# Moving the decoding of the second network's weights from steps 15 to 59 to steps 60 to 95

## The chip, the core and the metric

The kernel runs on one core of a Trainium2 chip. The core has five engines that run beside each other, each through its own list of instructions in order: TensorE (PE in the rows, with its weight loads as PEld), VectorE (DVE), ScalarE (ACT), GpSimd (POOL) and SyncE (SP), which issues most DMA transfers. Time is device time in microseconds from one launch. The kernel before took 1014.66 us, the median of three runs (1014.65, 1014.66 and 1016.03 us).

## What is computed

Four sequences of 4224 tokens with 192 channels go through three layers, shortened here from the reference:

```
x  = causal convolution of x, 7 taps per head, softmax weights       # 8 heads of 24 channels
u  = x + ((x^T @ U) @ V)^T                                           # rank 32, along the sequence
x  = u + max(u @ w_ch1, 0) @ w_ch2                                   # first network, 192 -> 768 -> 192
u  = x + real(fft over tokens and channels of x)
un = (u - mean(u)) / sqrt(var(u) + 1e-6)
y  = u + max(un @ moe2_w_ch1, 0) @ moe2_w_ch2                        # second network, same sizes
```

All inputs arrive as 64-bit floats. A weight is therefore loaded as two 32-bit words and decoded on the chip, scaled by the largest absolute value, and split into a high and a low 16-bit part. Products are formed from high x high, high x low and low x high.

## The kernel before

**Blocks and steps.** A sequence is cut into 11 blocks of 384 tokens. Each block goes once through the first network and once through the second, which gives 88 blocks; their order over (network, sequence) is (0,0), (0,1), (0,2), (1,0), (0,3), (1,1), (1,2), (1,3). So blocks 0 to 32 use the first network, and block 33 is the first that needs the weights of the second. A block i is worked in three steps, 3i, 3i+1 and 3i+2. In each step two of the six 128-row parts of layer 1 are issued (`layer1`, L665 and L655: five matmuls a part, then the eviction `hh` on ACT at L650 and the residue `hl` on VectorE at L651), and one third of layer 2 of the block before (`layer2`, L697 to L701, 18 matmuls, added to the result by VectorE at L704).

**Paired blocks.** In blocks 5 to 10, 22 to 33 and 76 to 87 all six parts of layer 1 are issued in the first step, and the six evictions follow together. All matmul results use one ring of eight PSUM buffers, taken in turn. After the six parts of layer 1 only two buffers are left, so the third group of matmuls after them waits until the first `hl` of the block has been written.

**Preparing the next input.** While block i runs, the input of block i+2 is prepared. VectorE adds a product (L525 or L534), takes maxima (L712) and scales (`cmax`, `rc`, L547 and L550); ACT scales and rounds (`un` L555, `sp` L578); GpSimd subtracts (`sp` L561); a transposing DMA issued by SP (L585) writes `ch`, which the matmuls at L665 read. In the paired stretches ACT's share of this stands between `rc` and the evictions of the next block.

**Background work.** Other work is written as lists of small functions, here called units. A table of windows `[a, z, units]` spreads the n units of a list over steps a to z-1: unit k is issued at the end of step a + floor(k (z-a) / n). Units of one step are issued in the order of the table: tables, weights of the second network (`weights_units(1)`), convolution of sequence 2 (`conv_units(2)`), the transform of sequence 0 (`fft_units`), and so on. An engine meets a unit's instructions at that place of its list and can't pass them by.

**The units that the change touches.** `weights_units(1)` first issues three DMA loads of 2.3 MB together (L201, `load`), then twelve decodes (`dec`: five VectorE instructions at L172 to L179 on 128x192 words, and a maximum at L223), and between and after them the scaling (L230 to L250) and the splits (L255, L262 on GpSimd, copies at L286 to L296). `conv_units` for sequences 2 and 3 loads its input in halves (`load_x`, L159), convolves (L398) in place, and ends with a scaling of its rank-32 product (`gsplit`). In the first list of `fft_units` a unit of kind a holds fold(c+1) and the matmuls s33(c,0), a unit of kind m holds split33(c+1) and s33(c,1); gathers of rows (`loadx`, indirect DMAs of GpSimd at L756) go with both. Fold is three instructions of VectorE (L790 to L793) and one of GpSimd (L795). Split33 is two of ACT (L802, L803) and one of GpSimd (L804), which s33 (L823) waits for. The two writers of `z` behind s33, ACT at L830 and VectorE at L831, wait for each other in turn where a unit writes `z` twice.

Of the kernel before, what the change touches and what calls it, by code (L numbers as in the profile page):

```python
# [19 lines left out]
FF = 768  # L20
# [77 lines left out]
def build(tc, io):  # L98
# [30 lines left out]
    with tc.manual_schedule():  # L129
# [59 lines left out]
        def weights_units(i):  # L189
            st = {}  # L190
            FH = FF // 2
            NW = FF + FH + NM * D
# [33 lines left out]
            def scale(n):  # L226

                mx = st["mx"]
                o, c = (0, len(pieces[0])) if n == 0 else (len(pieces[0]), len(pieces[1]))
                nc.vector.tensor_reduce(out=mx[:, 16 + n:17 + n], in_=mx[:, o:o + c], axis=AX.X,  # L230
                                        op=ALU.max)
# [72 lines left out]
            def decs(n):  # L304
                o = len(pieces[0]) if n else 0
                return [lambda q=q, e=e: dec(*q, o + e) for e, q in enumerate(pieces[n])]

            if i == 0:
                st["part"] = load_part
                w0_st.update(st=st)  # L310
            return [load] + decs(0) + [lambda: scale(0), lambda: scale2(0),
                                       lambda: scaled(0, FF + FH, 0), split1h, split1e, split1a, split1b] + \
                   decs(1) + [lambda: scale(1), lambda: scale2(1),
# [16 lines left out]
        def gsplit(b, gf):  # L330

            st = {}

            def size():
                gm = st["gm"] = wrk.tile([P, 4], F32, name="gm", bufs=2)
                nc.vector.tensor_reduce(out=gm[:, 0:1], in_=gf(), axis=AX.X, op=ALU.max,
                                        apply_absolute_value=True)

            def scale():
                gm = st["gm"]  # L340
                all_max(gm[:, 1:2], gm[:, 0:1])
                nc.vector.tensor_scalar(out=gm[:, 1:2], in0=gm[:, 1:2], scalar1=1e-30,
                                        scalar2=1 / 64.0, op0=ALU.max, op1=ALU.mult)
                nc.vector.reciprocal(gm[:, 2:3], gm[:, 1:2])
                nc.vector.tensor_tensor(out=gm[:, 3:4], in0=gm[:, 1:2], in1=vsc[:, 0:1],
                                        op=ALU.mult)

            def split():
                gm = st["gm"]
                g = wrk.tile([P, D], F16, name="gst", bufs=2)  # L350
                nc.scalar.activation(g[:96], gf()[:96], AF.Identity, scale=gm[:96, 2:3])
                nc.vector.scalar_tensor_tensor(out=g[64:96], in0=gf()[64:96],
                                               scalar=gm[64:96, 2:3], in1=g[64:96],
                                               op0=ALU.mult, op1=ALU.subtract)
                gst[b] = g, gm

            return [size, scale, split]

        def conv_units(b):
            st = {}  # L360
# [79 lines left out]
            if not b:  # L440
                return out

            return out + [lambda f=f: (f(), stored and stored.pop(0)())
                          for f in gsplit(b, lambda: st["g"])]

        def z_tile():
# [278 lines left out]
        def fft_units(b):  # L725
# [6 lines left out]
            def scale():  # L732

                m = xmax[b]
                nc.vector.tensor_reduce(out=m[:, 11:12], in_=m[:, 0:NB], axis=AX.X, op=ALU.max)
# [177 lines left out]
                nc.gpsimd.tensor_tensor(out=y1, in0=y1, in1=near(1, 1), op=ALU.add)  # L913

            last = len(chunks) - 1
            first = [lambda: (scale(), loadx(0)), scale2, lambda: (fold(0), loadx(1)), lambda: split33(0), None]
            for c in range(len(chunks)):
                a, m = [lambda c=c: s33(c, 0)], [lambda c=c: s33(c, 1)]
                if c < last:
# [100 lines left out]
        def play(t):  # L1020
            for q in START[t].split() if t < len(START) else ():
                if q in jobs:
                    jobs[q]()
                else:
# [13 lines left out]
        ft = [fft_units(b) for b in range(B)]  # L1038

        windows = [[28, 32, [load_tables]],  # L1040
                   [15, 60, weights_units(1)],
                   [25, 57, [lambda: load_x(2, 0, 0), lambda: load_x(2, 0, 1), None] + conv_units(2)],
                   [37, 70, ft[0][0]], [70, 100, ft[0][1]],
                   [98, 127, ft[1][0]], [125, 153, ft[1][1]],
# [93 lines left out]
```

## Time and profile before

| what | value |
| --- | --- |
| median of three runs | 1014.66 us |
| profiled execution, span from the first to the last instruction | 1017.3 us |
| profiled execution, a time of its own beside the span | none is given |
| TensorE busy | 979.1 us, 96% of the span |
| VectorE busy | 748.4 us, 74% |
| ScalarE busy | 604.4 us, 59% |
| GpSimd busy | 380.9 us, 37% |
| mean granted clock of TensorE | 0.992 |

The profile is of one execution. A row's times count from the start of its span. Its busy shares are averages over stretches that have different limits, so the table says only that TensorE comes first. Where it stood idle, and for whom, is in the rows further below.

### The profile page before, as it was taken

The page shows a single profiled execution, that of the slowest core. Times are in us where ns is not written, and L with a number is a line of the kernel's source. Part 1 is how long each engine was busy: PE and PEld are TensorE (multiplying, and loading weights), DVE is VectorE, ACT ScalarE, POOL GpSimd, SP SyncE. Part 2 cuts the span into 40 slices and gives each one's busy share as a digit, 9 for nine tenths or more (in the row PEclk, how much of TensorE's full clock was granted, in tenths as well). Part 3 has the DMA queues.
Part 4 walks back from the last instruction along what each step waited for, and adds up shares of the span by engine and source line. Part 5 has one row for each costly group of instructions (what it writes and reads, how often), then busy time and mean ns, then how long its engine had stood idle before and what let it go on. Part 6 is the DMA issues. An engine that isn't in the chain of part 4 may idle for free.

```text
span 1017.3 us, 25682 instructions
## 1 busy us (share of the span) xinstructions
PE 979.1 (96%) x9929; PEld 764.8 (75%) x9929; DVE 748.4 (74%) x2094; ACT 604.4 (59%) x1512; POOL 380.9 (37%) x397
## 2 busy tenths in 40 slices
PE   8789898999899999999999999998999999999998
PEld 5466676777677777877778887776888877877776
DVE  7766577689876656687776777897789787766663
ACT  2556554765676666656576666655656665555552
POOL 0111111253552344265534445564157651562110
PEclk9999999999999999999999999999999999999999
DMA  7596857685536666443425455433344332542332
GB/s 288 155 230 183 252 148 189 178 213 158 151 99 154 203 201 179 114 138 101 102 73 146 134 155 139 108 87 82 87 131 110 107 87 65 137 110 68 82 72 63
DMA packets 190804, 139.28 MB, mean 137 GB/s; under 512 B 128186, under 2 KB 164257, under 8 KB 189913
## 3 DMA queue, kind: packets, MB, share of 16 engines
q1 hardware_dynamic: 183095, 124.59, 45.6%
q0 software_dynamic: 7104, 12.70, 4.8%
q8 instruction: 77, 1.26, 0.5%
q14 instruction: 46, 0.38, 0.1%
q10 hardware_dynamic: 482, 0.35, 0.1%
HBM read 61.69 MB, written 46.11 MB: 106 GB/s over the span
## 4 chain that ended last, share of the span: by engine, by line
PE 62%; DVE 12%; DMA 11%; POOL 5%; issue 5%; ACT 4%; SPq 0%; DVEq 0%; ACTq 0%; POOLq 0%
PE l L665 24%; PE l L697 9%; PE l L701 8%; PE l L699 8%; PE l L655 5%; DMA ch<-sp 4%; DVE hl L651 3%; DMA xm<-x2d,mrow 2%; POOL xm L756 2%; PE cv L398 2%; PE sd L863 2%; PE s L879 2%; DMA x1d<-xw 1%; DVE x L790 1%; POOL xp L804 1%
## 5 line engine op out<-in xcount | busy, mean ns | idle before, releaser
L665 PE MATMUL l<-ch,w1h 128*128 128x384 f16 x1584 | 407.2, 327 | 15.4 <-DMA ch<-sp 10.1
L697 PE MATMUL l<-w2h,hh 128*128 128x192 f16 x1584 | 391.9, 247 | 5.8 <-DVE hl L651 4.5
L699 PE MATMUL l<-w2l,hh 128*128 128x192 f16 x1584 | 391.4, 247 | 1.2 <-DVE w2l L264 1.2
L701 PE MATMUL l<-w2h,hl 128*128 128x192 f16 x1584 | 391.4, 247 | 0.5 <-DVE hl L651 0.4
L651 DVE SCALAR_TENSOR_TENSOR hl<-l,hh 128x384 f16<-128x384 f32 x528 | 267.6, 549 | 127.2 <-ACT hh L650 126.1
L650 ACT ACTIVATE hh<-l 128x384 f16<-128x384 f32 x528 | 235.3, 494 | 155.7 <-PE l L655 155.3
L665 PEld LDWEIGHTS <-w1h 128*128 128x128 f16 x1584 | 155.1, 98 | 106.8 <-DMA ch<-sp 12.3
L697 PEld LDWEIGHTS <-hh 128*128 128x128 f16 x1584 | 155.6, 98 | 23.1 <-issue 12.3
L665 PE MATMUL l<-ch,w1l 128*128 128x384 f16 x528 | 172.7, 327 | 0.0
L699 PEld LDWEIGHTS <-hh 128*128 128x128 f16 x1584 | 155.7, 98 | 17.1 <-issue 6.5
L701 PEld LDWEIGHTS <-hl 128*128 128x128 f16 x1584 | 155.7, 98 | 3.1 <-DVE hl L651 1.4
L561 POOL TENSOR_TENSOR sp<-un,sp 128x576 f16<-128x576 f32 x44 | 57.3, 1302 | 250.4 <-ACT sp L578 228.3
L655 PE MATMUL l<-ch,w1l 128*128 128x384 f16 (+1 forms) x528 | 133.9, 327 | 0.0
L756 POOL DMA_INDIRECT xm<-x2d,mrow x84 | 84.9, 1011 | 21.3 <-issue 17.8
L631 POOL TENSOR_TENSOR sp<-un,sp 128x576 f16<-128x576 f32 x34 | 44.9, 1320 | 120.2 <-ACT sp L578 118.9
L625 ACT ACTIVATE un<-u,mr,rs 128x192 f32<-128x192 f32 x132 | 62.4, 537 | 25.3 <-DVE mr L619 24.7
L555 ACT ACTIVATE un<-u,rc 128x192 f32<-128x192 f32 x132 | 50.2, 445 | 43.0 <-DVE rc L550 43.0
L704 DVE SCALAR_TENSOR_TENSOR u<-l,cmax,u 128x192 f32<-128x192 f32 x132 | 54.5, 413 | 25.5 <-PE l L701 20.9
L665 PEld LDWEIGHTS <-w1l 128*128 128x128 f16 x528 | 51.8, 98 | 28.0 <-issue 4.0
L543 ACT ACTIVATE junk<-u 128x192 f16<-128x192 f32 x132 | 47.7, 361 | 40.6 <-DVE u L534 24.2
L849 POOL DMA_INDIRECT u<-x2d,mrow x64 | 62.4, 975 | 15.3 <-issue 11.7
L704 DVE SCALAR_TENSOR_TENSOR u<-l,ws,u 128x192 f32<-128x192 f32 x132 | 53.9, 410 | 18.2 <-PE l L701 18.0
(136 smaller groups left out, 1189.5 us busy)
## 6 DMA issues: line engine op xcount, KB each, us to landing
x2d<-u SPq DMA_DIRECT2D x68, 288.0 KB
u<-x1d SPq DMA_DIRECT2D x44, 288.0 KB
out_d<-u SPq DMA_DIRECT2D x43, 288.0 KB
x1d<-xw SPq DMA_DIRECT2D x36, 210.0 KB
u<-x2d SPq DMA_DIRECT2D x32, 192.0 KB
x<-x2d SPq DMA_DIRECT2D x60, 99.0 KB
xw<-x_d SPq DMA_DIRECT2D x4, 1344.0 KB
xw<-x_d SPq DMA_DIRECT2D x8, 672.0 KB
```

What stands on the lines that cost most here:

```text
L561: low_engine(0, b, j).tensor_tensor(out=sp[:, :, D:2 * D], in0=k["un"], in1=sp[:, :, :D], op=ALU.subtract)
L625: nc.scalar.activation(un[:, t], u[:, t], AF.Identity, scale=k["r"][:, t:t + 1], bias=k["m"][:, t:t + 1])
L650: nc.scalar.activation(hh[:, m], acc[m], AF.Relu)
L651: nc.vector.scalar_tensor_tensor(out=hl[:, m], in0=acc[m], scalar=0.0, in1=hh[:, m], op0=ALU.max, op1=ALU.subtract)
L655: nc.tensor.matmul(acc[m].rearrange("p (r n) -> p r n", r=TB), lhsT=w["l1"][rows, n, m * P:(m + 1) * P], rhs=kd[x][rows], start=False, sto ...
L665: nc.tensor.matmul(o, lhsT=w[v][:, e, ms], rhs=kd[x], start=(n == 0), stop=False)
L697: nc.tensor.matmul(o, lhsT=hh[:, m, rs], rhs=w["h2"][:, m], start=(m == 0), stop=False)
L699: nc.tensor.matmul(o, lhsT=hh[:, m, rs], rhs=w["l2"][:, m], start=False, stop=False)
L701: nc.tensor.matmul(o, lhsT=hl[:, m, rs], rhs=w["h2"][:, m], start=False, stop=(m == NM - 1))
L704: nc.vector.scalar_tensor_tensor(out=u[:, r], in0=o, scalar=sc, in1=u[:, r], op0=ALU.mult, op1=ALU.add)
L756: nc.gpsimd.indirect_dma_start(out=xs[c][1][:, g], out_offset=None, in_=x2d[b][:], in_offset=bass.IndirectOffsetOnAxis(ap=mrow[:99, k:k + ...
L849: nc.gpsimd.indirect_dma_start(out=u2[:, s0 + 2 * e], out_offset=None, in_=src[:], in_offset=bass.IndirectOffsetOnAxis(ap=mrow[:, k2 + e - ...
```

## The change

Four edits. The window of the second network's weights becomes steps 60 to 95. Its units get a new order: four empty units behind the loads, the decodes of the second half between the later units of the first, and three empty units near the end; 24 units become 31. The scaling at the end of the convolution of sequences 2 and 3 gets two empty units, so that these two lists have 18 units for 16. In the first list of each transform an empty unit stands between finding the largest value and using it, which makes 18 units of 17. Nothing else is computed and nothing is left out.

```diff
@@ weights_units @@
+            if i:
+                d0, d1 = decs(0), decs(1)
+                return [load, None, None, None, None] + d0 + \
+                    [lambda: scale(0), d1[0], d1[1], lambda: scale2(0), d1[2],
+                     lambda: scaled(0, FF + FH, 0), split1h, split1e, d1[3], split1a, d1[4],
+                     split1b, d1[5], lambda: scale(1), None, None, lambda: scale2(1), None,
+                     lambda: scaled(FF + FH, NW, 1), split2]
             return [load] + decs(0) + [lambda: scale(0), lambda: scale2(0),
                                        lambda: scaled(0, FF + FH, 0), split1h, split1e, split1a, split1b] + \
                    decs(1) + [lambda: scale(1), lambda: scale2(1),
...
@@ gsplit @@
-            return [size, scale, split]
+            return [size, None, scale, None, split] if b > 1 else [size, scale, split]
...
@@ conv_units @@
-            return out + [lambda f=f: (f(), stored and stored.pop(0)())
+            return out + [lambda f=f: (f and f(), stored and stored.pop(0)())
...
@@ fft_units @@
-            first = [lambda: (scale(), loadx(0)), scale2, lambda: (fold(0), loadx(1)), lambda: split33(0), None]
+            first = [lambda: (scale(), loadx(0)), None, scale2, lambda: (fold(0), loadx(1)), lambda: split33(0), None]
...
@@ windows @@
-                   [15, 60, weights_units(1)],
+                   [60, 96, weights_units(1)],
```

By the rule for windows the loads move from step 15 to 60. The decodes stood at steps 16, 18, 20, 22, 24, 26, 41, 43, 45, 46, 48 and 50; now they stand at 65, 66, 68, 69, 70, 71, 73, 75, 77, 82, 84 and 86. The last split moves from step 58 to 94. Line numbers below the first edit grow by 7.

First place: VectorE in block 6 of the kernel before, from the copy of a convolution's product to the maximum at L712. `dec` is the decoder's scratch, `u_1474` the loaded weights, `l` a PSUM result of layer 2.

```order
L419 COPY gacc<-gp 128x192
L704 SCALAR_TENSOR_TENSOR u<-l_1505,cmax,u 128x192
L172 TENSOR_SCALAR dec<-u_1474 128x192
L175 TENSOR_SCALAR dec<-dec 128x192
L176 TENSOR_SCALAR dec<-dec 128x192
L178 SCALAR_TENSOR_TENSOR dec<-u_1474,dec 128x192
L179 SCALAR_TENSOR_TENSOR u_1474<-u_1474,dec 128x192
L223 TENSOR_REDUCE mx_1482<-u_1474 128x1
L122 TENSOR_REDUCE vsc<-am 128x1
```

The same place of VectorE in the changed kernel.

```order
L426 COPY gacc<-gp 128x192
L711 SCALAR_TENSOR_TENSOR u<-l_1495,cmax,u 128x192
L122 TENSOR_REDUCE vsc<-am 128x1
L471 TENSOR_SCALAR vsc<-vsc 128x1
L473 RECIPROCAL vsc<-vsc 128x1
L711 SCALAR_TENSOR_TENSOR u<-l_1536,cmax,u 128x192
L719 TENSOR_REDUCE xmax<-u 128x1
```

The first decode and its wait for the load are gone from the path to the maximum.

Second place: VectorE at the end of block 22 before, from the second third of layer 2 to the first `hl` of block 23.

```order
L704 SCALAR_TENSOR_TENSOR u<-l_4649,cmax,u 128x192
L534 SCALAR_TENSOR_TENSOR u<-h,gm,u 128x192
L704 SCALAR_TENSOR_TENSOR u<-l_4674,cmax,u 128x192
L712 TENSOR_REDUCE xmax<-u 128x1
L547 TENSOR_SCALAR cmax<-cmax 128x3
L550 RECIPROCAL rc<-cmax 128x3
L831 SCALAR_TENSOR_TENSOR z<-s_4699,z 95x34x3
L831 SCALAR_TENSOR_TENSOR z<-s_4699,z 95x34
L651 SCALAR_TENSOR_TENSOR hl<-l_4725,hh 128x384
```

The same place in the changed kernel, from the last third of layer 2 on.

```order
L711 SCALAR_TENSOR_TENSOR u<-l_4570,cmax,u 128x192
L719 TENSOR_REDUCE xmax<-u 128x1
L554 TENSOR_SCALAR cmax<-cmax 128x3
L557 RECIPROCAL rc<-cmax 128x3
L172 TENSOR_SCALAR dec<-u_4133 128x192
L175 TENSOR_SCALAR dec<-dec 128x192
L176 TENSOR_SCALAR dec<-dec 128x192
L178 SCALAR_TENSOR_TENSOR dec<-u_4133,dec 128x192
L179 SCALAR_TENSOR_TENSOR u_4133<-u_4133,dec 128x192
L223 TENSOR_REDUCE mx_4141<-u_4133 128x1
L838 SCALAR_TENSOR_TENSOR z<-s_4602,z 95x34x3
L838 SCALAR_TENSOR_TENSOR z<-s_4602,z 95x34
```

A decode now stands between `rc` and the two writes of `z` (step 68); another one, of step 66, stands ahead of these rows, behind the first third of layer 2.

Third place: SP's queue around the end of block 10 before. The second load of `xw` here is the second half of chunk 1 of sequence 2.

```order
L504 DMA u<-x1d_67 128x576
L159 DMA xw<-x_d 128x1344
L716 DMA x2d_70<-u 128x576
L504 DMA u<-x1d_67 128x576
L585 DMA_TRANSPOSE ch<-sp 128x9x128
L159 DMA xw<-x_d 128x1344
L716 DMA x2d_70<-u 128x576
```

The same place in the changed kernel.

```order
L511 DMA u<-x1d_67 128x576
L159 DMA xw<-x_d 128x1344
L723 DMA x2d_70<-u 128x576
L159 DMA xw<-x_d 128x1344
L511 DMA u<-x1d_67 128x576
L592 DMA_TRANSPOSE ch<-sp 128x9x128
L159 DMA xw<-x_d 128x960
```

The half moves up past one load of `u` and one transpose; it is issued at step 32 for 33 before, and the convolution that reads it is issued at step 33 for 35 before.

## Rows read from the trace of the kernel before

**Rows 1.** The page's first part: busy time, share of the span and instructions.
```profile
PE 979.1 (96%) x9929; PEld 764.8 (75%) x9929; DVE 748.4 (74%) x2094; ACT 604.4 (59%) x1512; POOL 380.9 (37%) x397
```
**Rows 2.** Timeline of TensorE: start, us, instruction, [idle before <-releaser]; five waits.
```profile
124.86 0.32 PE L697 MATMUL l<-w2h,hh 128*128 128x192 f16 x1 [3.37 <-DVE hl L651]
...
165.34 0.24 PE L697 MATMUL l<-w2h,hh 128*128 128x192 f16 x1 [1.16 <-DVE hl L651]
...
169.74 0.34 PE L665 MATMUL l<-ch,w1h 128*128 128x384 f16 x1 [1.18 <-DMA ch<-sp]
...
193.02 0.72 PE L398 MATMUL cv<-xw,tap 64*64 64x168 f32 x12 [1.03 <-DMA xw<-x_d]
...
267.08 0.50 PE L665 MATMUL l<-ch,w1h 128*128 128x384 f16 x1 [2.83 <-DMA ch<-sp]
```
**Rows 3.** Windows: us, busy PE, PEld, DVE, ACT, POOL (x), PEclk, DMA share, GB/s.
```profile
122.00:126.00 4.00, 1.14 (x8) 1.05 (x8) 1.75 (x4) 3.97 (x12) 1.27 (x1) 0.65 0.52 192
126.00:130.00 4.00, 4.00 (x36) 2.83 (x35) 3.19 (x7) 1.78 (x4) 0.26 (x1) 0.50 0.98 227
...
268.00:272.00 4.00, 4.00 (x30) 2.91 (x29) 1.80 (x7) 2.13 (x6) 0.61 (x1) 0.75 0.62 207
...
694.00:698.00 4.00, 4.00 (x27) 2.75 (x26) 1.80 (x4) 1.41 (x4) 1.83 (x2) 0.67 0.57 145
```
**Rows 4.** Timeline of VectorE: the wait for the load; start and end of one decode.
```profile
117.57 0.26 DVE L172 TENSOR_SCALAR dec<-u 128x192 int32<-128x192 int32 x1 [3.41 <-DMA u<-wa_d]
...
156.61 0.25 DVE L172 TENSOR_SCALAR dec<-u 128x192 int32<-128x192 int32 x1
...
158.54 0.28 DVE L122 TENSOR_REDUCE gm<-am 128x1 f32<-128x128 f32 x1
```
**Rows 5.** Timeline of ACT in block 9, behind that decode.
```profile
164.23 1.61 ACT L650 ACTIVATE hh<-l 128x384 f16<-128x384 f32 x4
```
**Rows 6.** Timeline of GpSimd ahead of the wait for `ch` at 267.08.
```profile
258.68 1.23 POOL L795 TENSOR_TENSOR xm<-x 99x380 f32<-99x380 f32 x1 [6.43 <-DVE xm L791]
...
262.44 1.30 POOL L561 TENSOR_TENSOR sp<-un,sp 128x576 f16<-128x576 f32 x1
```
**Rows 7.** Timeline of TensorE: waits in the transform of sequence 2.
```profile
678.71 0.48 PE L823 MATMUL s<-vt,xp 99*97 99x102 f16 x6 [1.16 <-POOL xp L804]
...
690.84 0.29 PE L823 MATMUL s<-vt,xp 99*97 99x102 f16 x2 [1.17 <-ACT xp L803]
692.56 0.62 PE L823 MATMUL s<-vt,xp 99*97 99x102 f16 x9 [1.43 <-POOL xp L804]
```
**Rows 8.** Timelines of SP's queue and of TensorE in block 11.
```profile
181.42 0.32 SPq L716 DMA_DIRECT2D x2d<-u  x1
...
187.93 0.58 SPq L159 DMA_DIRECT2D xw<-x_d  x1
...
184.14 0.72 PE L398 MATMUL cv<-xw,tap 64*64 64x168 f32 x12
```
**Rows 9.** Windows of 20 us, columns as in rows 3, in blocks 22 to 26.
```profile
320.00:340.00 20.00, 19.54 (x200) 15.19 (x198) 13.18 (x36) 12.33 (x38) 6.92 (x8) 1.00 0.68 178
340.00:360.00 20.00, 20.00 (x214) 15.26 (x215) 12.42 (x32) 14.45 (x42) 8.26 (x12) 1.00 0.57 179
```
**Rows 10.** Timelines of ACT, VectorE and TensorE between blocks 22 and 23.
```profile
323.42 0.32 ACT L830 ACTIVATE z<-s 95x34 f16<-95x34 f32 x1 [0.87 <-DVE z L831]
...
326.01 0.87 ACT L650 ACTIVATE hh<-l 128x384 f16<-128x384 f32 x2 [0.39 <-PE l L655]
...
326.53 2.88 DVE L651 SCALAR_TENSOR_TENSOR hl<-l,hh 128x384 f16<-128x384 f32 x6 [2.46 <-ACT hh L650]
...
327.90 0.25 PE L697 MATMUL l<-w2h,hh 128*128 128x192 f16 x1
```
**Rows 11.** Timelines of GpSimd and VectorE: a decode beside a GpSimd subtraction.
```profile
248.12 1.64 POOL L804 TENSOR_TENSOR xp<-xm,xp 99x768 f16<-99x768 f32 x1 [0.42 <-POOL sp L561]
...
248.15 1.72 DVE L176 TENSOR_SCALAR dec<-dec 128x192 int32<-128x192 int32 x1
```

## The prediction

> **What bounds the kernel now.** I read the page first, then TensorE's waits, then short windows around the long ones, and last the chains that led to them. The page gives TensorE 979.1 us of a span of 1017.3 us [rows 1], so the time can only fall where TensorE stands idle or runs at its lower clock. The waits tell where that is. Behind the start-up, the large ones of the first network lie in blocks 6 to 18: 3.37, 1.16, 1.18, 1.03 and 2.83 us [rows 2]. Those of the second network that matter here lie in blocks 55 and 56: 1.16, 1.17 and 1.43 us [rows 7]. A long wait costs twice. After the one of 3.37 us the granted clock is 0.65 and then 0.50 of full speed for 4 us each; after the one of 2.83 us it is 0.75, and after the pair in block 56 it is 0.67 [rows 3]. Half speed is the lower of the two levels, 1.2 GHz for 2.4. In blocks 22 to 26, into which the decodes move, TensorE is nearly full (19.54 and 20.00 of 20 us) and VectorE has about a third of the time free (13.18 and 12.42 busy) [rows 9].
>
> **What goes away.** The decode at 117.57 sat at the head of VectorE's queue for 3.41 us until its weights landed [rows 4]. Behind it waited the addition that frees layer 2's buffers, the scales, ACT's rounding, the evictions, and then TensorE for 3.37 us. This wait leaves that place with its decode. With it goes the slow clock: from 124.86 to 130 TensorE works 5.1 us at half speed [rows 2, 3], which loses 2.6. Sum 6.0 us.
>
> One decode holds VectorE from 156.61 to 158.54, that is 1.93 us [rows 4]. In block 9 it stands ahead of the scales, so `hh` comes at 164.23 [rows 5], TensorE waits 1.16 us for the residue and then 1.18 us for the next `ch` [rows 2]. Two microseconds earlier, both are covered: 2.3 us.
>
> The wait at 267.08 has a longer chain. GpSimd's fold stood 6.43 us waiting for VectorE, whose queue held a decode of 1.93 us ahead of the fold, and the subtraction that makes `ch` came behind it, at 262.44 [rows 6]. Without decodes the fold is earlier, and by the new step numbers (fold at step 51 for 50, the subtraction before it in that step) it no longer stands ahead of that subtraction. 2.83 us of wait, and 1.0 us for the 2 us at half speed in the window 268 to 272 [rows 3]: 3.8 us.
>
> In the transform of sequence 2 the old list had split33 and the s33 that reads it one step apart at steps 169 and 170, where 1.17 + 1.43 us were lost [rows 7]. With 18 units in 27 steps each unit m stands two steps ahead of the next a. The loss of 1.16 us a block earlier has the same cause, a late `xp`, but had two steps already. With the slow clock behind it (0.67 over 4 us is 2.6 us at half speed, 1.3 lost [rows 3]) 5.1 us are at stake, and I take 5.0. Gains together: 6.0 + 2.3 + 3.8 + 5.0 = 17.1 us.
>
> **What comes instead: the decodes in blocks 22 to 28.** Each one placed ahead of `rc`, or ahead of VectorE's part of `z`, delays ACT's rounding and so the evictions of the next block. ACT waited 0.39 us for TensorE ahead of them, and the first residue, about a sixth of 2.88 us after 326.53, was written near 327.05, while TensorE reached the matmul that needs its buffer at 327.90 [rows 10]: 0.85 us more. A delay of d costs TensorE d - 0.39 - 0.85. Block 22 has two such decodes, of steps 66 and 68. The second follows `rc`, but the row at 323.42 shows ACT waiting for VectorE between two writes of `z` [rows 10], and that pair is now behind it. So 3.9 - 1.24 = 2.7 us at the start of block 23. A wait of 2.83 us brought the low clock [rows 2, 3], so 1.4 us more, as after that wait. Block 23 has three decodes, two ahead of `rc`: 2.7 again, less 0.5 since a slower TensorE leaves VectorE time, 2.2. Block 24 has one: 0.7. The last five, the three scalings and splits on ACT and the subtractions on GpSimd lie in longer blocks with convolutions, where VectorE has 7.6 of 20 us free [rows 9]; I take 1.3. Bounds: nothing, if VectorE's free third covers all, and 12 x 1.9 = 23 us, if every decode were to lengthen TensorE's path by its whole length. I take 2.7 + 1.4 + 2.2 + 0.7 + 1.3 = 8.3, near the rows of block 9, where one decode cost 2.3.
>
> **The loads at step 60** share the DMA engines with `ch` of block 21, whose transpose is issued ahead of them. Before, they ran without a wait for `ch` on TensorE; I take 0.3 us (0 to 2). The first decode now comes five steps later than they, so it does not wait.
>
> **The convolution of sequence 2.** The half of its input that the convolution in block 11 needs is issued earlier in SP's list, right behind the store at 181.42 instead of at 187.93; there it landed just ahead of 193.02, 5 us later [rows 2, 8]. So it lands near 187, and later if the store ahead of it counts. But the convolution itself moves up two steps, to the place at 184.14 [rows 8]. TensorE waits about 3.1 us for 1.03 before, and may fall to the low clock (half of 1.6): 2.1 + 0.8 = 2.9 us.
>
> **The other transforms.** For sequence 0 the distances stay two steps. Sequence 1 keeps two places with one step. Sequence 3 had none and gets three (202 to 203, 205 to 206, 208 to 209). Such a place cost 2.60 us at step 170 [rows 7]; three others of before show little. Bounds 0 to 7.8; I take 1.5.
>
> **Sum.** Losses 8.3 + 0.3 + 2.9 + 1.5 = 13.0, gains 17.1: 4.1 us less. The profiled execution has no time beside its span of 1017.3, which lies 2.6 above the median; the difference carries over: 1014.66 - 4.1 = 1010.6 us.
>
> **A rule that speaks against the change.** Beside a GpSimd subtraction that began at 248.12, an instruction of a decode took 1.72 us [rows 11], where the first of a decode without such a neighbour took 0.25 [rows 4]. The Trainium skill ("SBUF — State Buffer", section "SBUF: two separate sides") says that the ports GpSimd shares with VectorE are an exclusive lock: whoever begins first keeps it to its end, and the other waits. The trace agrees. Taken over to all decodes it makes the rival named third below.
>
> **Rivals.** First, VectorE's free third hides the decodes: the losses fall to 0.3 + 2.9 + 1.5 = 4.7 us. That gives 1014.66 - 17.1 + 4.7 = 1002.3. For it: 6.8 us of 20 free [rows 9]; against: block 9 did not hide one. Second, gains and losses cancel: only the wait for the load goes (6.0), and the fold and the transforms find new late steps, at 1014.5. For it: those chains pass GpSimd, which the change relieves little. Third, GpSimd holds the decodes: the last five lie where it works 8.26 us of 20 [rows 9]; 1.72 - 0.25 = 1.5 us each, half of it on TensorE's path, makes 3.7 us more, 1014.3. Fourth, slower: the delay does not die out in block 24. If decodes come faster than VectorE catches up, every block from 23 to 29 waits 2 to 3 us as block 23 does, and three of these waits bring the low clock: 7 x 2.5 + 3 x 1.4 = 21.7 for 8.3, so 1024. It decides from the point where two neighbouring blocks each wait over 3 us. A mild form (15 us) gives 1017. That the weights come too late for block 33 is no rival: the last split stands five steps ahead of it.
>
> **How the numbers follow.** Chances: forecast 0.42, hidden 0.18, cancelled 0.15, held by GpSimd 0.08, slower 0.17. The forecast's own range is 1006 to 1014. The range that should hold 8 in 10 is 1002.5 to 1017.5: it reaches into the hidden case and takes the mild form of the slower one. About 0.2%, 2 us, can be told from no change. Faster takes nearly all of the forecast, the hidden case and some of the held one: 0.62. Same, 0.19, takes the cancelled case and edges. Slower 0.19.
>
> **What would show it.** The 3.37 us wait and the low clock after it gone, and TensorE's waits in blocks 9, 10 and 17 too: gains right. A wait for `hl` of 2 to 4 us at the start of block 23 and one of about 2 in block 24, with `un` late behind `z`: the main loss right. A wait of about 3 us for `xw` in block 11. No two waits for `xp` in block 56. The forecast is wrong if block 23 does not wait, if block 11 does not, or if VectorE's backlog lasts beyond block 25.

## The result and the profile after

The changed kernel takes 1020.07 to 1021.8 us, median 1020.13. Beside it the kernel before took 1015.35 (1014.65 to 1017.76). The ratio is 1.0052, 95% interval [1.0036, 1.0068]: some 5 us slower, where 4 us faster was forecast.

The page of the changed kernel, against [rows 1]:

```profile
PE 979.4 (96%) x9929; PEld 763.0 (75%) x9929; DVE 740.5 (73%) x2094; ACT 605.1 (59%) x1512; POOL 378.9 (37%) x397
```

The work is the same, so the time lies in waits again. What was to go did go. Windows in block 6 and behind the old wait for `ch`, columns as in [rows 3], of the changed kernel:

```profile
122.00:126.00 4.00, 3.78 (x51) 3.33 (x48) 3.09 (x7) 1.55 (x8) 0.26 (x1) 1.00 0.92 271
126.00:130.00 4.00, 4.00 (x30) 2.64 (x29) 1.42 (x4) 2.56 (x9) 0.00 (x0) 1.00 0.56 122
268.00:272.00 4.00, 4.00 (x43) 3.15 (x42) 2.06 (x5) 3.94 (x9) 2.92 (x2) 1.00 0.46 137
```

The clock is 1.00 where it was 0.65, 0.50 and 0.75. In blocks 55 and 56 no wait for `xp` above 0.5 us is left of [rows 7]. Of the waits that answer to [rows 2], the largest that remains in blocks 9 to 11 is the one for `xw`:

```profile
177.18 1.43 PE L405 MATMUL cv<-xw,tap 64*64 64x168 f32 x32 [0.77 <-DMA xw<-x_d]
```

What was to come came too. Timelines of VectorE, ACT and TensorE between blocks 22 and 23, against [rows 10]; the two rows of VectorE are the first instruction of a decode and the write of `z` behind it:

```profile
310.60 0.23 DVE L172 TENSOR_SCALAR dec<-u 128x192 int32<-128x192 int32 x1
...
312.50 0.30 DVE L838 SCALAR_TENSOR_TENSOR z<-s,z 95x102 f16<-95x102 f32 x1
```

```profile
308.06 0.32 ACT L837 ACTIVATE z<-s 97x34 f16<-97x34 f32 x1 [4.11 <-DVE z L838]
...
312.84 0.32 ACT L837 ACTIVATE z<-s 95x34 f16<-95x34 f32 x1 [2.80 <-DVE z L838]
...
314.94 1.23 ACT L657 ACTIVATE hh<-l 128x384 f16<-128x384 f32 x3
```

```profile
316.05 0.32 PE L704 MATMUL l<-w2h,hh 128*128 128x192 f16 x1 [2.16 <-DVE hl L658]
...
327.78 0.33 PE L537 MATMUL h<-gst,vst 96*128 96x192 f16 x2 [0.86 <-DVE rp L876]
...
328.78 0.24 PE L704 MATMUL l<-w2h,hh 128*128 128x192 f16 x1 [0.68 <-DVE hl L658]
```

Twice ACT waits between two writes of `z` for VectorE, which is decoding; its evictions come late and TensorE waits 2.16 us for a residue.

The surprise is in blocks 67 to 69, the transform of sequence 3. There TensorE was busy 39.84 of 40 us in the kernel before (windows, columns as in [rows 3]):

```profile
798.00:812.00 14.00, 14.00 (x149) 11.42 (x148) 10.09 (x29) 10.36 (x22) 9.80 (x10) 1.00 0.37 99
812.00:824.00 12.00, 12.00 (x130) 10.03 (x128) 8.32 (x26) 7.61 (x18) 8.75 (x8) 1.00 0.56 119
824.00:838.00 14.00, 13.84 (x145) 11.04 (x143) 12.29 (x33) 7.67 (x17) 6.63 (x8) 1.00 0.24 64
```

TensorE's timeline in the changed kernel:

```profile
803.82 0.29 PE L830 MATMUL s<-vt,xp 99*97 99x102 f16 x2 [0.55 <-ACT xp L810]
806.14 0.67 PE L830 MATMUL s<-vt,xp 99*97 99x102 f16 x10 [2.03 <-POOL xp L811]
...
819.02 0.67 PE L830 MATMUL s<-vt,xp 99*97 99x102 f16 x10 [0.55 <-POOL xp L811]
...
830.23 0.29 PE L830 MATMUL s<-vt,xp 99*97 99x102 f16 x2 [0.67 <-ACT xp L810]
...
831.96 0.67 PE L830 MATMUL s<-vt,xp 99*97 99x102 f16 x10 [1.43 <-POOL xp L811]
```

Five waits for `xp`, 5.2 us in all (2.58 us at the first of the three one-step places, 0.55 at the second, 2.10 at the third), and behind the largest the low clock (windows, the same kernel):

```profile
803.00:807.00 4.00, 1.43 (x18) 0.92 (x16) 2.41 (x8) 3.97 (x9) 3.49 (x4) 0.98 0.39 112
807.00:811.00 4.00, 4.00 (x22) 2.54 (x21) 0.40 (x1) 1.37 (x3) 2.56 (x3) 0.59 0.33 112
```

At 0.59 over 4 us, 3.3 us ran at half speed, which loses 1.6 us. With the waits that is 6.9 of the 7.7 us by which blocks 63 to 71 are longer.

The table gives the length of stretches of blocks in us, each block from TensorE's first layer 1 matmul to that of the next block. The runs named e... are described below. "Before" is the trace shown ahead of the prediction.

| blocks | before | e1 (before again) | after | e2 | e9 | e10 | e11 | e16 |
| --- | --- | --- | --- | --- | --- | --- | --- | --- |
| 5-19 | 187.5 | 182.9 | 174.6 | 175.1 | 188.6 | 187.1 | 186.8 | 174.5 |
| 22-24 | 30.1 | 30.2 | 37.2 | 37.2 | 31.6 | 31.7 | 31.6 | 37.3 |
| 25-32 | 91.9 | 91.9 | 97.7 | 97.7 | 93.0 | 93.0 | 93.9 | 97.8 |
| 33-41 | 96.7 | 96.8 | 93.1 | 94.0 | 93.4 | 92.4 | 92.9 | 93.1 |
| 50-57 | 89.5 | 88.9 | 86.8 | 89.6 | 88.7 | 86.2 | 86.4 | 86.7 |
| 63-71 | 94.8 | 94.4 | 102.5 | 94.4 | 94.6 | 94.7 | 94.7 | 94.9 |

### The profile page after: what moved, and what is told of

Same layout as the page of the kernel before. It is cut to its first block, busy times and chain, and to the rows that moved or that the text cites. A ratio compares the mean times of both kernels' runs of the same rounds, so it can differ in the third digit from the quotient of the medians.

```text
span 1018.3 us, 25681 instructions
## 1 busy us (share of the span) xinstructions
PE 979.4 (96%) x9929; PEld 763.0 (75%) x9929; DVE 740.5 (73%) x2094; ACT 605.1 (59%) x1512; POOL 378.9 (37%) x397
## 5 line engine op out<-in xcount | busy, mean ns | idle before, releaser
L662 PEld LDWEIGHTS <-w1l 128*128 128x128 f16 (+1 forms) x528 | 40.5, 97 | 34.5 <-issue 9.9
```

Source lines behind the costliest of these rows:

```text
L662: nc.tensor.matmul(acc[m].rearrange("p (r n) -> p r n", r=TB), lhsT=w["l1"][rows, n, m * P:(m + 1) * P], rhs=kd[x][rows], start=False, sto ...
```

## The experiments

Each ratio is to the kernel before, run on the same chip at the same time. e5 to e8 ran on a chip where that kernel took 1028.09 us; in the other groups it took 1015.76 to 1017.25. An interval reaches some 1.5 us to either side (2.4 at most), so the difference of two ratios is known to 2 or 3 us. Lengths of blocks are from one trace of each kernel.

**e1: the kernel before once more.** Nothing edited; it shows how far one trace of it can be trusted.

> The kernel before, unchanged, as a control. Two theories. T1: the trace of before shows what all its runs do, and the change lost its gains in the transform of sequence 3, where the empty unit put split33 and the s33 that reads it one step apart at three places. T2: the trace of before is of an execution slower than most (its span of 1017.3 is above its median of 1014.66), the gains read from it in blocks 5 to 19 are partly not there in other runs, and the moved decodes cost more than they free. T1: a span of 1017 again, ratio 1.000. T2: a span near 1013, ratio 1.000, with blocks 5 to 19 some 3 to 5 us shorter than in the first trace.

0.9997 [0.9982, 1.0012], runs from 1012.45 to 1017.99 us; the profiled span is 1010.7 where the first was 1017.3. At the place of the 3.37 us wait in [rows 2] this execution has

```profile
122.06 0.24 PE L697 MATMUL l<-w2h,hh 128*128 128x192 f16 x1 [1.90 <-DVE hl L651]
```

and the clock behind it is 1.00 for 0.50. The wait belongs to the kernel, its size and the slow clock to the execution. Block 18 says the same of the clock: the wait for `ch` comes again, with 2.86 us at 262.71, and the clock stays at 1.00 where it was 0.75. Both theories are half right: the span was that of T2, the loss in sequence 3 that of T1 (e2).

**e2: no empty unit in the transforms.** The rest of the change is kept.

```diff
-            first = [lambda: (scale(), loadx(0)), None, scale2, ...
+            first = [lambda: (scale(), loadx(0)), scale2, ...
```

> The changed kernel with the empty unit in the transforms' first list taken out again (17 units as before); the moved decodes and the scaling's empty units stay. T1: sequence 3 gives 8 us back, and sequences 1 and 2 lose what they had gained (2 to 5): 1014 to 1018 us, no waits for xp of 0.5 us or more in blocks 66 to 69. T2: it stays at 1018 to 1021.

0.9992 [0.9977, 1.0008]: the loss is gone, and blocks 63-71 are back at 94.4. So the empty unit costs some 6 us net (1.0052 - 0.9992), and all else in the change saves 0.8, which can't be told from nothing.

**e3: the window of sequence 3 two steps longer.** The changed kernel's one-step places in it (202 to 203, 205 to 206, 208 to 209) all become two steps; the units stand at other steps of their blocks.

```diff
-                   [190, 215, ft[3][0]], [219, 237, ft[3][1]]]
+                   [190, 217, ft[3][0]], [219, 237, ft[3][1]]]
```

> The changed kernel with the window of sequence 3's first list ending two steps later (217 for 215): 27 steps for 18 units, as sequence 2 has, so that no s33 stands one step behind its split33; nothing else differs. T1: the waits for xp in blocks 66 to 70 go, and the low clock behind them: 1020 - 8 = 1012 us. T2: under 2 us gained, 1018 or more.

0.9998 [0.9983, 1.0012], blocks 63-71 98.2. That takes 5.5 us off the changed kernel, of the 10 that sequence 3 costs it (e16), and 4.3 of 7.6 in this trace. Three waits for `xp` stay, of 0.74, 1.38 and 0.71 us, though every distance is two. Timelines of ACT and GpSimd ahead of the first:

```profile
807.27 0.84 ACT L810 ACTIVATE xp<-xm 99x768 f16<-99x768 f32 x1
```

```profile
808.79 1.29 POOL L638 TENSOR_TENSOR sp<-un,sp 128x576 f16<-128x576 f32 x1
810.04 1.64 POOL L811 TENSOR_TENSOR xp<-xm,xp 99x768 f16<-99x768 f32 x1
```

At all three places GpSimd makes the subtraction for the next input (`sp`) between ACT's part of the split and its own, so these splits take 5.38, 5.37 and 4.71 us where those of the kernel before took 4.14, 4.14 and 3.53. So the step of the block at which a chain stands counts too.

**e4: the empty unit alone, on the kernel before.**

```diff
-            first = [lambda: (scale(), loadx(0)), scale2, ...
+            first = [lambda: (scale(), loadx(0)), None, scale2, ...
```

> The kernel before with the transforms' empty unit alone; decodes stay in steps 15 to 59. T1: 8 us lost in sequence 3, 2 to 5 us gained in sequences 1 and 2: 1017 to 1021 us. T2: no difference, within 2 us of before.

1.0039 [1.0017, 1.0061], blocks 63-71 104.7. It makes the loss without the weights, as T1 had it.

**e5: the weights alone**, their new list and window on the kernel before.

```diff
-                   [15, 60, weights_units(1)],
+                   [60, 96, weights_units(1)],
...
+            if i:
+                d0, d1 = decs(0), decs(1)
+                return [load, None, None, None, None] + d0 + ...
```

> The kernel before with the move of the weights and their new order alone: no empty units in the transforms or in the scaling of sequences 2 and 3. Theory A: the move is worth nothing because it gives back in blocks 22 to 32 what it frees in blocks 5 to 19 (about 9 us each): within 2 us of before, with blocks 22 to 24 together 7 us longer. Theory B: the move itself is good and the scaling's empty units, which shift convolutions of sequences 2 and 3, cost: 3 us or more faster than before.

1.0011 [0.9994, 1.0027]: no change that can be told, as theory A had it. Blocks 22-24 are 36.4 and 25-32 97.0.

**e6: as e5, the weights last in the table of windows**, so that a decode comes behind the other units of its step.

> As the run with the weights alone, but the weights' window stands last in the table, so that in a step that has both, the decode comes behind the transform's writes of z (steps 66 and 68) and behind its additions. Theory A with the pair of z as the cause: the wait at the start of block 23 (2.6 us and the low clock) falls to 1 us or less, 3 to 4 us faster than the run with the weights alone. Rival: only VectorE's total counts, and the delay shows up in block 24 instead: within 1.5 us of it.

1.0027 [1.001, 1.0043]. Against e5, blocks 22-24 fall to 34.5, but 25-32 rise to 100.9: the delay goes elsewhere, as the rival said.

**e7: as e6, one decode at the last step of each block** from step 59 to 92 (the load at 54).

```diff
+                at.update(zip(range(59, 95, 3), d0 + d1))
+                return [at.get(t) for t in range(54, 97)]
```

> The same decodes at one place in each block from 19 to 30: the last step, behind rc and everything else of that step, where VectorE waits 2 to 3 us for the first eviction of the next block (steps 59, 62, ..., 92; load at 54). Theory A (what costs is a decode ahead of rc, not its 1.93 us): blocks 20 to 32 within 3 us of the kernel before, blocks 5 to 19 about 8 us shorter, 1007 to 1010 us. Rival (VectorE's work in these blocks is too much wherever it stands): blocks 20 to 32 stay 8 us or more longer, 1014 or more.

1.0016 [0.9992, 1.0039]. Blocks 22-24 are 31.1, so one decode in a block can nearly be hidden there. Blocks 20 to 32 together take 152.7 us, some 10 above the kernel before (142.9, on another chip), so the rival held; blocks 12-19 are 4 us longer than in e5 (97.3 for 93.3) and 20-21 2.8 (23.6 for 20.8). That the earlier load does this is likely and not shown.

**e8: the changed kernel with the empty unit for sequence 2 alone.**

```diff
+            first = [lambda: (scale(), loadx(0))] + [None] * (b == 2) + [scale2, ...
```

> The changed kernel with the transforms' empty unit for sequence 2 alone. The spacing theory: blocks 50 to 57 are 2.5 us shorter than without it, blocks 63 to 71 as before: 1012.5 to 1014.5. Rival (the even spacing does not matter, the first trace of before had an unlucky pair of waits): as without any, 1015 to 1016.

0.9959 [0.9946, 0.9973]. Against e2 the empty unit of sequence 2 gives 3.4 us; against the changed kernel the ones of sequences 0, 1 and 3 cost 9.4. Both compare ratios from different chips; e10 and e16 repeat them elsewhere.

**e9: the scaling's empty units alone**, on the kernel before.

```diff
-            return [size, scale, split]
+            return [size, None, scale, None, split] if b > 1 else [size, scale, split]
```

> The kernel before with only the empty units of the scaling (sequences 2 and 3); weights and transforms as before. Theory A: these units, not the move of the weights, give most of the gain left in blocks 12 to 19 and 33 to 41; so about 5 us faster (ratio 0.993 to 0.997), blocks 12-19 about 90 us (before 94.6 to 96), blocks 33-41 about 94 (before 96.7), blocks 22-32 as before, 122. Rival B: the gain needs the weights out of blocks 5 to 19 as well; then these units alone give 0 to 1 us and 12-19 stays at 94.

0.9997 [0.9984, 1.001]; blocks 5-19 stay at 188.6. The theory fell: the gain there needs the weights moved. Blocks 33-41 are 3.3 us shorter and 22-32 are 2.6 longer: work moved forward.

**e10: e9 and the empty unit for sequence 2**, the weights where they were.

> The kernel before with the scaling's empty units and the transform's empty unit for sequence 2 alone; the weights stay in steps 15 to 59. Theory A: the move of the weights is worth about nothing, so this stands about 3 us below the kernel with the scaling's units alone, some 7 to 8 us under the kernel before (ratio 0.991 to 0.994), blocks 50-57 at 86 to 87 for 89. Rival B: without the moved weights it is no more than 3 us faster (0.997 or above).

0.9959 [0.9947, 0.9971], 3.9 us under e9 on the same chip. The same as e8, which has the weights moved. Theory A was right on the step from e9, and wrong on the 7 to 8 us in all, since e9 gave nothing.

**e11: e8 with the load and the decodes back at their old steps**, scalings and splits at the new ones.

```diff
+                at.update(zip((16, 18, 20, 22, 24, 26, 41, 43, 45, 46, 48, 50), decs(0) + decs(1)))
+                return [at.get(t) for t in range(15, 95)]
```

> The changed kernel with the transform's empty unit for sequence 2 alone, and the load and the twelve decodes back in the steps they have in the kernel before; the scalings and splits of the weights stay in steps 72 to 94. It tells the decodes from the scalings and splits. Theory A: the decodes cause the 7 us in blocks 22-24 (30 again for 37) and at least 4 of the 6 us in blocks 25-32 (93 to 94 for 97.7). Rival C: the scalings and splits on ScalarE, VectorE and GpSimd cause what blocks 25-32 lose: they stay at 96 to 98, and only 22-24 fall. In blocks 5-11 the wait for the load may come back (up to 6 us).

0.9983 [0.9969, 0.9997]. Blocks 22-24 are 31.6 and 25-32 93.9: the decodes cause 5.6 us in the first and 3.9 in the second stretch, the scalings and splits 0.9. The gain in blocks 5-19 is gone (186.8), with a wait of 2.41 us for `hl` in block 6.

**e12: e10 with three empty units behind the load**, at the old place.

```diff
-            return [load] + decs(0) + [...
+            return [load] + [None] * (3 * i) + decs(0) + [...
```

> The kernel before with the scaling's empty units, the transform's empty unit for sequence 2 alone, and three empty units between the weights' load and their first decode, all in steps 15 to 59. Theory A: the only loss that the old place of the weights must have is the wait for their load; with that wait covered this is the fastest of the four, 0 to 5 us under the same kernel without the three units, ratio 0.987 to 0.993. Rival D: the wait for the load was a matter of single executions, and the later decodes press on block 15 to 19 instead; then it is the same or up to 3 us slower than without them.

1.0026 [1.0012, 1.0041], 6.8 us over e10. Blocks 5-11 gain 1.8, and 12-19 lose 6.1: the rival had the place, with more than twice the 3 us that it allowed. Waits in blocks 14 and 17:

```profile
226.30 0.24 PE L530 MATMUL h<-gst,vst 96*128 96x192 f16 x1 [2.63 <-DVE hl L651]
...
258.34 0.50 PE L665 MATMUL l<-ch,w1h 128*128 128x384 f16 x1 [2.61 <-DMA ch<-sp]
```

**e13: the changed kernel with every s33 of sequence 3 two steps behind its split.** The empty unit stays. The folds and gathers that share a unit with an s33 move with it.

```diff
+            if b == 3:
+                at = dict(zip((190, 192, 194, 195, 198, 199, 201, 202, 204, 205, 207, 208, 210, 211, 213, 214), [f for f in first if f]))
+                first = [at.get(t) for t in range(190, 215)]
```

> The changed kernel with its empty unit kept in all four transforms, but sequence 3's units put by hand: the three s33 that stood one step behind the split they read (203, 206, 209) one step later, and the last units with them, so that every s33 stands two steps behind its split. Theory A (distance): the waits for xp in blocks 67 to 69 go, blocks 63-71 fall from 102.5 to 95 us, and the kernel comes out some 7 us under the changed one, ratio to the kernel before 0.995 to 0.998. Rival B (the later start of the whole list, its folds and gathers, is what costs): blocks 63-71 stay above 98 and the ratio at 1.002 or more.

0.9979 [0.9967, 0.9991], blocks 63-71 96.4 (1.5 above e16), no wait for `xp` above 0.1 us left, and the clock is full:

```profile
803.00:807.00 4.00, 4.00 (x40) 3.17 (x37) 3.24 (x12) 3.78 (x8) 3.48 (x4) 1.00 0.40 114
807.00:811.00 4.00, 3.98 (x42) 3.19 (x42) 2.72 (x11) 3.17 (x8) 3.49 (x4) 1.00 0.35 114
```

**e14: the kernel before with three s33 of sequence 3 one step earlier**, one behind their splits, again with the folds and gathers of their units.

```diff
+            if b == 3:
+                at = dict(zip((190, 191, 192, 194, 197, 198, 200, 201, 202, 204, 205, 207, 208, 210, 212, 213), [f for f in first if f]))
```

> The kernel before, without any of the change, but with three s33 of sequence 3 one step earlier (202, 205, 208 for 203, 206, 209), one step behind the splits at 201, 204 and 207; nothing else moves. Theory A (distance): this alone makes 6 to 9 us in blocks 63-71 (101 to 104 for 94.6), ratio 1.006 to 1.009. Rival B: the place alone costs what the prediction took, up to 2.6 us for one of them, 1.5 in all: ratio below 1.003.

1.0056 [1.0036, 1.0076]; blocks 63-71 99.0, under what was expected, with waits of 1.55 and 0.80 us for `xp`. Shorter distances slow the kernel, with none of the change in it. At the second and third place `sp` stands inside the split again, as in e3, so not all of it is the distance.

**e15: the changed kernel with two buffers for `xp`.**

```diff
-                t = wrk.tile([99, 2, XG * D], F16, name="xp", bufs=1)
+                t = wrk.tile([99, 2, XG * D], F16, name="xp", bufs=2)
```

> The changed kernel with two buffers for xp where it has one. With one, ScalarE may write the next xp only when TensorE is done with the second s33 of the chunk before, which stands in the same step; then GpSimd's 1.64 us follow. Theory A: that round trip is why one step is too short; with a second buffer the split runs ahead of that s33, TensorE's waits for xp fall to under 0.5 us each, blocks 63-71 come to 95 to 97 us for 102.5, ratio 0.995 to 0.999. Rival C: the split is late for another reason (gather, fold and sum ahead of it on GpSimd), and a second buffer changes less than 2 us.

1.0061 [1.0047, 1.0075], blocks 63-71 102.4, with the same five waits. The theory of the one buffer fell.

**e16: the changed kernel without the empty unit in sequence 3.**

```diff
+            first = [lambda: (scale(), loadx(0))] + [None] * (b < 3) + [scale2, ...
```

> The changed kernel with the transform's empty unit for sequences 0, 1 and 2, and not for 3. Theory A: sequence 3 alone makes the loss: ratio 0.995 to 0.997, within 1.5 us of the kernel with the empty unit for sequence 2 alone. Rival B: sequences 0 and 1, which have one-step places of their own, cost 2 us or more: ratio 0.998 or above.

0.9952 [0.9936, 0.9969], the lowest ratio of all. Sequences 0 and 1 cost nothing that can be told.

**e17: e16 with the weights where they were.**

> The kernel before with the scaling's empty units and the transform's empty unit for sequences 0 to 2; the weights stay in steps 15 to 59. Against the run e16, which differs by the move of the weights alone, it prices that move. Theory A: gains in blocks 5 to 19 and losses in 22 to 32 cancel; ratio 0.994 to 0.998, within 2.5 us of that run. Rival B: the move is a gain of its own that shows once the transforms are mended; ratio 0.998 or above.

0.9957 [0.9942, 0.9972]: within some 2 us the move of the weights is worth nothing, with all else at its best. In the two traces it gains 10.9 us in blocks 5-19 (185.4 here) and costs 5.6 in 22-24 and 4.8 in 25-32.

**e18: the changed kernel, the last operation of the split on VectorE in sequence 3.**

```diff
-                nc.gpsimd.tensor_tensor(out=t[:, 1, :n], in0=x, in1=t[:, 0, :n], op=ALU.subtract)
+                (nc.vector if b == 3 else nc.gpsimd).tensor_tensor(
+                    out=t[:, 1, :n], in0=x, in1=t[:, 0, :n], op=ALU.subtract)
```

> The changed kernel with the split's last operation, the subtraction that fills the second half of xp, on VectorE for sequence 3 instead of GpSimd; the short distances stay. Theory A: a split takes ScalarE 0.94 and 0.84 us and then GpSimd 1.66 behind a gather of 1.0 us, which is a whole step of some 3.5 us; with VectorE in GpSimd's place it ends 1 to 1.5 us sooner, so blocks 63-71 fall from 102.5 to 96 to 99 us, ratio 0.998 to 1.002. Rival C: the split begins late on ScalarE (behind the evictions and the fold), and VectorE's queue is as late as GpSimd's: blocks 63-71 stay above 100 and the ratio above 1.003.

0.9987 [0.9972, 1.0002]; blocks 63-71 98.3. With distances as short as in the changed kernel, a faster split takes back 6.5 us by time and 4.2 in this trace. TensorE's waits there:

```profile
804.76 0.29 PE L831 MATMUL s<-vt,xp 99*97 99x102 f16 x2 [0.72 <-ACT xp L810]
805.83 0.67 PE L831 MATMUL s<-vt,xp 99*97 99x102 f16 x10 [0.77 <-DVE xp L811]
```

## Why the prediction was wrong

**The step that failed** is the term for the other transforms: "Such a place cost 2.60 us at step 170; three others of before show little. Bounds 0 to 7.8; I take 1.5." The places were the right ones, and the mechanism, a late `xp`, was right; the size was not. Between e16 and the changed kernel, which differ in sequence 3 alone, lie 1.0% of the time, 10 us (8 to 12 by the two intervals), and 7.6 us in the traces of blocks 63-71. That is at the upper bound or beyond it, though not as three places of 2.60: two cost as much or nearly (2.58 and 2.10 us of waits), the second 0.55, and and the low clock 1.6. The row that was nearest to the case was at hand and was set aside for places of which no row was shown.

That it is the distance, for the most part, is shown from three sides: restored, 7 of 10 us by time go (e13; 5.5 in e3); made without the change, a loss of 5.7 us comes (e14); with a quicker split at the same distance, 6.5 go (e18). In e13 and e14 folds and gathers move too; e18 moves nothing. The place in the block counts beside it, as e3 shows. Timelines of ACT and GpSimd in the changed kernel say why one step does not do:

```profile
801.95 0.94 ACT L809 ACTIVATE xm<-xm,xmax 99x768 f32<-99x768 f32 x1 [3.05 <-POOL xm L802]
802.92 0.84 ACT L810 ACTIVATE xp<-xm 99x768 f16<-99x768 f32 x1
```

```profile
803.41 1.00 POOL L763 DMA_INDIRECT xm<-x2d,mrow  x1 [0.30 <-issue]
804.43 1.66 POOL L811 TENSOR_TENSOR xp<-xm,xp 99x768 f16<-99x768 f32 x1
```

A split goes through ACT (0.94 and 0.84) and GpSimd (1.66), which is 3.44 us, and here GpSimd was still issuing a gather when ACT was done: from 801.95 to 806.09 it took 4.14. The kernel before needs the same 4.14 us for this split, and ACT waits for the fold there too. Its ACT, GpSimd and TensorE:

```profile
804.34 0.94 ACT L802 ACTIVATE xm<-xm,xmax 99x768 f32<-99x768 f32 x1 [2.07 <-POOL xm L795]
...
806.83 1.66 POOL L804 TENSOR_TENSOR xp<-xm,xp 99x768 f16<-99x768 f32 x1
...
809.83 0.72 PE L823 MATMUL s<-vt,xp 99*97 99x102 f16 x12
```

What differs is when TensorE comes to the s33. At the three places it came 5.5, 4.3 and 3.2 us behind the start of the split in the kernel before, and 1.3, 2.8 and 1.2 us behind it in the changed kernel, where the splits took 4.14, 3.59 and 3.53 us. A step of block 68 in the kernel before is 10.44 / 3 = 3.48 us, so one step less takes most of the room away. With VectorE for GpSimd the last part took 0.96 us and the split 2.87 (e18). A second buffer (e15) changes nothing in this chain.

The one-step places that cost little can be read the same way. At step 110 of the changed kernel TensorE came 3.6 us behind the start of a split of 3.59 us, and did not wait; at step 123 the split is that of the last, smaller chunk, 2.37 us long, and the waits were 0.51 and 0.92 us. In the kernel before, the three others of the prediction show waits of 0, 0.53 and 0 us (steps 109, 116 and 173). Why a split starts earlier in one step than in another is open; no run changed that.

**The weights and the scaling.** Their sum was forecast as 12.1 gained and 11.5 lost, 0.6 us to the good; e2 measures 0.8 (-0.8 to 2.3). That the sum agrees is luck, since the parts do not:

- The gains in blocks 5 to 19 were 12.1, less 2.9 for the wait for `xw`. Seven traces with the weights at the old place average 186.6 us (before, e1, e4, e9, e10, e14, e17; 182.9 to 189.9), and seven with the weights and the scaling changed 174.6 (after, e2, e3, e13, e15, e16, e18; e8, on the chip of e5 to e7, has 178.0). So 12.0, which single traces of the old kernels would put anywhere from 8 to 15. Of the 12.1, 2.6 and 1.0 were slow clock, which e1 does not have. No term was given to decodes that GpSimd held before: three of their instructions took 1.21, 1.21 and 1.72 us there (at 233.42, 246.61 and 248.15), beside GpSimd's subtractions. The term of 2.9 was wrong: the wait for `xw` is 0.77 where it was 1.03 [rows 2]. The half was issued right behind the store, as forecast (172.52 behind 172.15), but TensorE came to the convolution 4.3 us behind the start of that store and not 2.7.
- Blocks 22 to 24 were to lose 7.0. They are 7.1 longer, of which 1.5 is the scaling's moved work (e9) and 5.6 the decodes (e11). The chain is the one described, `z` and then the evictions, and it dies out in block 24 as far as TensorE's long waits go. The 1.4 us of slow clock were put down as those behind the wait of 2.83 us, where the prediction itself had read 1.0; here the clock was 0.65 from 316 to 320, which does lose 1.4. The decode of step 65, in block 21, had no term and cost nothing that can be seen: blocks 21 and 22 take 10.14 and 10.44 us in e2 as before. Nor did the loads at step 60, put at 0.3: blocks 20 and 21 together are 20.8 in both. (The first residue of [rows 10] comes near 327.01 by the prediction's own sum, not 327.05, which changes nothing.)
- The last five decodes, scalings and splits were put at 1.3 and cost 4.7 (97.7 against 93.0 in e9); e11 puts 3.9 of it on the decodes. Here the backlog does last beyond block 25, one of the prediction's own signs of being wrong, though in waits of about a microsecond or less (the longest 1.16, in block 29).
- The scaling's empty units had no term but `xw`. They make blocks 33 to 41 3.3 us shorter (e9), about as much as the term above was short.
- GpSimd hardly held the decodes. The instruction that took 1.72 us in [rows 11], at all its twelve places from 296 to 400 us of the changed kernel, with the lowest, median and highest ns:

```profile
L176 DVE TENSOR_SCALAR dec<-dec x12: 259/260/261, 298.3 to 388.1; 128x192 int32<-128x192 int32 x12
```

The exclusive lock of which the Trainium skill speaks ("SBUF — State Buffer", section "SBUF: two separate sides") shows in [rows 11]. At the new place the longest instruction of any decode took 0.57 us where the others of its line took 0.36 to 0.40 (L179, at 372.19, beside a GpSimd subtraction).

**The transform of sequence 2.** 5.0 forecast; 3.4 (e8 against e2) and 3.9 (e10 against e9) measured. Both waits in block 56 went, and with them the slow clock behind them, which six of the eight traces with the old spacing have (before, e1, e2, e5, e7, e9; e6 and e14 have the waits without it). What the 5.0 left out is a longer wait of layer 1 at the start of block 53: 1.65 us in the changed kernel, 0.98 to 1.55 in e4, e10, e13 and e16, for 0.38 before.

**The sum** as measured: -0.8 for weights and scaling, -3.4 for sequence 2, +9.4 for the other transforms, +5.2 us. (The three are differences along a chain of kernels from before to after, so they add up whatever they are.) Two of the three terms lay within 2 us of the forecast; the third was 8 off. Among the rivals the cancelling one was right for the weights; none had the transforms on its side. The slower one had its place in blocks 23 to 29 and was to lose 21.7 us there; these blocks are 10.6 us longer than with the scaling's units alone (e9), nearer to the forecast's 8.3. The time came out slower, which the prediction gave a chance of 0.19, by a path that it had not taken for the danger.

## What to carry to other kernels

When units are spread over steps by a rule, list the distance between each producer and its consumer before and after, for every list that the rule spaces anew, and hold it against the time that the producer needs on its engines. Better than steps is time: read from the trace how long behind the producer's start the consumer comes. An empty unit that widens one distance shortens another. Where a row of the trace prices such a place and a count says how often it now occurs, the product is the estimate until other rows are shown against it. Work taken from one full stretch to another is worth nothing until a run shows that the new stretch has room: moving twelve decodes gained 12 us and cost 10.

## What was not expected of the hardware

One kernel's executions spread over 1012.45 to 1017.99 us on one chip, and two profiles of it differ by 6.6 us (1017.3 and 1010.7). A part of that is the granted clock: behind a wait of 3.37 us it was 0.50 for 4 us, behind one of 1.90 us at the same place it stayed at 1.00. The length of a wait does not settle it: behind 2.83 us it was 0.75, behind 2.86 us at the same place in e1 1.00, and behind 2.16 us in the changed kernel 0.65. A slow stretch can also be regular: the one behind block 56's waits came in six of eight traces. On another chip the kernel before took 1028.09 us, and all four kernels there took 99.7 us or more for blocks 63-71, with sequence 3's list as before; the same list gave 94.4 to 94.9 on the others. The waits for `xp` there stand at the same three places, two steps behind their splits: 1.15, 0.83 and 0.43 us in e5. In the kernel before TensorE waited 0.16 us at the third of them. So the old list is close to its edge as well; why it is passed on that chip is open.
